# Seven-product operands of w_out2: made in tiles 1 to 10 of the first layer instead of in tile 11 and pair 0; two splits moved at each pair's end

## The chip, the cores and the metric

The kernel runs on one core of a Trainium2 chip. The metric is the device time of one execution in microseconds (us), and of several runs the median. A core has five engines with an instruction queue each, which are told apart by the names of the profile: PE (TensorE, matrix products; PEld are its weight loads), DVE (VectorE), ACT (ScalarE), POOL (GpSimd) and SP (SyncE, which issues all the DMA transfers of this kernel). Each queue is worked off in order; engines wait for each other by semaphores.

## What is computed

A small attention, a gated layer and a second layer with a leaky activation, over 8 x 576 = 4608 tokens of width 512, all in float32:

```python
p_packed = sm_attn(p, k, v)                 # 8 batches, 8 heads, 32 packed keys, head width 64
out = sm_attn(q, p_packed, p_packed)        # 576 tokens a batch
x = out.transpose(0, 2, 1, 3).reshape(4608, 512)
xn = x / sqrt(mean(x * x) + 1e-6) * rms_g
y = (silu(xn @ w_gate) * (xn @ w_val)) @ w_out          # 1536 hidden
h = y @ w_in2                                           # 2048 hidden
result = (maximum(h, 0) + alpha * minimum(h, 0)) @ w_out2
```

## The kernel before

**Precision.** A float32 operand is split in two float32r halves: `split_hi` (ACT, line 110) rounds it, `split_lo` (DVE, line 113) subtracts the rounded part. A product is then three matmuls (`mm3`, lines 121 to 124). In the profile the halves are `hh`/`hl`, `yh`/`yl`, `in_h`/`in_l`, `wgh`/`wgl`.

**First layer, tiles 0 to 11.** Tokens go in 12 tiles (variable `c`, line 949) of 512 (tiles 0, 4, 7, 10; "wide") or 320 (the others; "narrow"). Each tile walks 12 blocks `f` of the hidden width. A block is: product g (`blk_in`), Tanh on ACT and `s` on DVE (lines 1075, 1080; both read PSUM), product v, `s` times v (line 1084), `hsplit`, then the output product of the block before (`blk_out(f - 1)`) and the operand of the next one (`both`: `in_h` on ACT; `in_l` on POOL at line 385 in tiles 1 to 6, and loaded from memory at line 383 from tile 7 on). Between these stand bits of the attention of later tiles (`work(f, at)` with `at` from 1 to 4, and `burst`): transposes, maxima, exponentials. g, v and the attention share four PSUM banks in turn.

**The weights of the second layer.** `w_in2` and `w_out2` arrive with a representation that must be narrowed first (`narrow`: two operations on DVE, one on ACT, an addition on POOL of line 234). The second layer multiplies 2x2 blocks with seven products instead of eight, so that of each of the 8 block pairs of either matrix seven operands are needed, blocks and their sums and differences, each split and stored to memory (`sevenths`, line 290: seven products, that is a split on ACT, a split on DVE and a store from one of two buffers `w7o`, and four combinations on DVE at line 305; it gives way after each of its four steps). The generator `late` (`conv_late`) narrows all pairs, makes the operands of `w_in2` and stores the narrowed `w_out2` raw. It is called in `work(f, 3)` of tiles 1 to 10, lines 980 to 982: after each odd block of a narrow tile, after each block of a wide one, and twice for each fourth block there. The generator `making` (`make_o7`) loads the raw pairs of `w_out2` again and makes their operands: one step ahead of each block of tile 11 (line 1069), and in pair 0 of the second layer three steps in each turn (`make`, lines 1250, 1262, 1272).

**Second layer, pairs 0 to 4.** Each pair (variable `pr`, line 1219) has two rows of 512 tokens (pairs 0 to 2) or 384 (pairs 3 and 4). A turn `i` of 8 has seven products into three banks, whose sums and activations run on DVE (lines 1157, 1160, 1169) and ACT (lines 1164, 1165), and two output blocks out of a list `fill` of pieces that TensorE does later (blocks "a" and "c" of each turn; a block is 12 matmuls of 256 columns at 512 tokens). The 40 other output blocks and the last "c" block, c4, wait in the list `LATER` until the turns are over; the first three of it are b5 of turn 0, b5 of turn 1 and c4 of turn 7. `block` is a generator: its first step splits on ACT, its second on DVE and puts the matmuls into `fill`. At the end of the turns `next(splits[0])` and the loop over `LATER` (lines 1357 to 1374) split each block one ahead of its matmuls. Between them run `prep` of the next pair (lines 868 to 905, from `y_raw` loads) and the sums of the results. `load_next` streams the stored operands, one load for each that was used.

Of the kernel before, what the change touches and what calls it, by code (L numbers as in the profile page):

```python
# [8 lines left out]
F32 = mybir.dt.float32  # L9
F32R = mybir.dt.float32r  # L10
# [8 lines left out]
def attention_moe_moe2_kernel(ctx, tc, q, k, v, p, w_gate, w_val, w_out, rms_g, w_in2, w_out2, alpha, out):  # L19
    nc = tc.nc  # L20
# [5 lines left out]
    T = 512  # L26
# [14 lines left out]
    NST = 4  # L41
# [49 lines left out]
    y_dram = tc.dram_tile([KD, 128, NT], F32, name="y_dram")  # L91
    gv_dram = tc.dram_tile([NJ * 4, 128, 512], F32, name="gv_dram")
    lo_dram = tc.dram_tile([NF, 128, 512], F32, name="lo_dram")
    w_dram = tc.dram_tile([NP2, 128, 2, 512], F32, name="w_dram")
    w7_dram = tc.dram_tile([NP2 * 7, 128, 2, 256], F32, name="w7_dram")
    o7_dram = tc.dram_tile([NP2 * 7, 128, 2, 256], F32, name="o7_dram")

# [28 lines left out]
    with tc.manual_schedule():  # L126
# [124 lines left out]
        def conv_late():  # L251
            ahead = [load_wide(u, one, NST) for u in units2[:2]]
            yield
            for m in range(0, len(units2), 2):
                pair = []
                for n in (m, m + 1):
                    pair.append(one.tile([128, 4, 128], F32, tag="w32", name="w32", bufs=2))
                    steps = narrow(ahead.pop(0), pair[-1])
                    next(steps)
                    yield  # L260
                    for _ in steps:
                        pass
                    if n + 2 < len(units2):
                        ahead.append(load_wide(units2[n + 2], one, NST))
                kind, i = units2[m]
                if kind == "o2":
                    for e in range(2):
                        nc.sync.dma_start(out=w_dram[i, :, e], in_=pair[e].rearrange("p c x -> p (c x)"))
                yield
                if kind == "i2":  # L270
                    yield from sevenths(kind, i, [t.rearrange("p c x -> p (c x)") for t in pair])

        def make_o7():
            def raw_pair(i):
                t = one.tile([128, 2, 512], F32, tag="w64", name="o2_raw", bufs=NST)
                nc.sync.dma_start(out=t, in_=w_dram[i])
                return t

            ahead = [raw_pair(0)]
            yield  # L280
            for i in range(NP2):
                t = ahead.pop(0)
                for n, _ in enumerate(sevenths("o2", i, [t[:, e] for e in range(2)])):
                    if n == 1 and i + 1 < NP2:
                        ahead.append(raw_pair(i + 1))
                    yield

        seventh_tags = [["w7o"]]

        def sevenths(kind, i, pair):  # L290
            blocks = [t[:, h * 256:(h + 1) * 256] for t in pair for h in range(2)]
            b11, b12, b21, b22 = blocks
            kept = w7_dram if kind == "i2" else o7_dram

            def products(*which):
                for n, src in which:
                    tags = seventh_tags[0]
                    t = one.tile([128, 2, 256], F32R, tag=tags[0], name="w7o", bufs=2)
                    tags.append(tags.pop(0))
                    split_hi(t[:, 0], src)  # L300
                    split_lo(t[:, 1], src, t[:, 0])
                    nc.sync.dma_start(out=kept[i * 7 + n], in_=t.bitcast(F32))

            def combine(out, x, y, op=ALU.subtract):
                nc.vector.tensor_tensor(out=out, in0=x, in1=y, op=op)

            if kind == "i2":
                products((0, b11), (1, b12))
                yield
# [639 lines left out]
        for c, (t0, n, cuts) in enumerate(CH):  # L949
# [9 lines left out]
            def work(f, at):  # L959
                live = [ch for ch in chains["k"] if ch.kind is not None][:1] + chains["q"]  # L960
                swap = c > 0 or at == 3 and any(ch.kind == X or ch.kind == M for ch in live)
                if swap and c == 0:
                    preload(ACTF.Exp)
                for ch in live:
                    n_ = 0
                    while n_ < 2:
                        if ch.kind == R and (at == 1 or at > 2 and (ch is first[0] or n_ == 0)):
                            pass
                        elif n_ == 0 and ch.kind == E and (c == 0 or at < 4) or swap and ch.kind in (X, M):
                            pass  # L970
                        else:
                            break
                        ch.last = (c, f, at)
                        ch.next()
                        n_ += 1
                if swap and c == 0:
                    preload(ACTF.Silu)
                if c == 0:
                    conv(2 if at < 4 else 0)
                elif not last and at == 3 and (f % 2 or n == T):  # L980
                    for _ in range(1 + (n == T and f % 4 == 3)):
                        next(late, None)

            def q_turn(now, free):
                for n_, ch in enumerate(chains["q"]):
# [64 lines left out]
            for f in range(NF):  # L1050
# [9 lines left out]
                if last:  # L1060
                    if f == 0:
                        y_rows.append(load_rows(0, 0))
                        prepare = prep(0)
                        making = make_o7()
                    if f > 0:
                        next(prepare, None)
                    if f in (2, 3, 8, 9, 10):
                        next(prepare, None)
                    next(making)
                    if f > 2:  # L1070
                        load_next()
                tg = blk_in(f, 0, "g")
# [22 lines left out]
                    work(f, 4)  # L1095
                if f < NF - 1:
                    both(("o", f + 1))
            tail = [NF - 2, NF - 1]
            if nq:
                for ch in chains["q"]:  # L1100
# [29 lines left out]
            if c == NP1 - 2:  # L1130
                ap_ctx.close()
                p2 = ctx.enter_context(tc.tile_pool(name="p2", bufs=1, side="right", reuse_waits="tile"))
                for _ in late:
                    pass

# [45 lines left out]
                for x in "hl"  # L1181
            ]

        seventh_tags[0] = ["w7o", "w32"]
        acc = {}

        def make(pr, i):
            if pr == 0 and i < NP2 - 1:
                next(making, None)

        def banks(x, j):
            if (x, j) not in acc:
# [26 lines left out]
        for pr, (t0, w) in enumerate(PAIRS):  # L1219
# [4 lines left out]
            def copies(to, x, w=w):  # L1224
                for j, m in pieces(w):
                    to[j] = temp(m)
                    evac(to[j], banks(x, j)[:, 0:m], True)

            for i in range(NP2):
                if i == NP2 - 2 and not final:  # L1230
                    y_rows.append(load_rows(pr + 1, 0))
# [15 lines left out]
                for f_ in waiting:  # L1247
                    f_()
                prod(c_, 4, True)
                make(pr, i)  # L1250
                prod(b_, 6, False)
                u3 = temp(w)
                add2(u3, m1, b_)
# [5 lines left out]
                prelu(g11, n11, i)  # L1259
                n22 = halves_of(h22, h22, w)  # L1260
                prelu(h22, n22, i + NP2)
                make(pr, i)
                fill.pop(0)()
                prod(c_, 2, False)
                h12 = temp(w)
# [1 line left out]
                then = (lambda f_=copies, to=m1s: f_(to, "a")) if i == NP2 - 1 else None  # L1267
                for _ in block("a", 0, i, g11, w, i == 0, i == NP2 - 1, then):
                    pass
                n12 = halves_of(h12, h12, w)  # L1270
                prod(b_, 3, False)
                make(pr, i)
                h21 = keep(1, i, w)
                add2(h21, m1, b_)
                prelu(h12, n12, i)
                s1 = temp(w)
                add2(s1, h12, h22)
                s2, s3 = keep(2, i, w), keep(3, i, w)
# [2 lines left out]
                n21 = halves_of(h21, h21, w)  # L1281
                late_h[i] = (h22, h21, s2, s3)
                fill.pop(0)()
                waiting = [
                    lambda h=h21, n=n21, f=i + NP2: prelu(h, n, f),
                    lambda s=s1, i=i, w=w: list(block("c", 4, i, s, w, i == 0, i == NP2 - 1)),
# [51 lines left out]
                    after.pop(0)  # L1338

            prepare = iter(()) if final else prep(pr + 1)  # L1340
            splits = []
            for x, n, i in LATER:
                h22, h21, s2, s3 = late_h[i]
                g = {5: s2, 2: s2, 6: s3, 3: h22, 1: h21, 4: s1}[n]
                then = None
                if n == 4:
                    then = lambda: copies(m5s, "c")
                elif i == NP2 - 1:
                    then = {5: done_b6, 2: done_c, 6: done_b7, 3: done_d, 1: done_a}[n]
                splits.append(block(x, n, i, g, w, n in (5, 3) and i == 0, i == NP2 - 1, then))  # L1350

            def combine_next(k_):
                if k_ < len(LATER) and LATER[k_][1] == 2:
                    _, h21, s2, _ = late_h[LATER[k_][2]]
                    less2(s2, h21, s2)

            next(splits[0])
            for k_ in range(len(LATER)):
                combine_next(k_ + 2)
                if k_ + 1 < len(LATER):  # L1360
                    next(splits[k_ + 1])
# [46 lines left out]
```

## Time and profile before

| | us |
|---|---|
| three runs | 1677.40, 1678.57, 1680.42 |
| median | 1678.57 |
| the profiled execution | 1682.31 |
| its span, first to last instruction | 1680.5 |
| PE busy / DVE busy / ACT busy / POOL busy | 1587.7 / 1198.7 / 894.5 / 206.3 |
| tiles 1 to 10, by the profile | 167.4 to 870.1 |
| tile 11 | 870.1 to 932.0 |
| pairs 0, 1, 2, 3, 4 begin at | 932.0, 1110.7, 1270.4, 1430.8, 1554.9 |
| from one 128x256 matmul of an output block to the next (1212.83, 1212.95, 1213.07) | 0.12 |

All times inside the profiled execution count from its first instruction. A stage is told by the first Tanh of its tile (line 1075) or the first copy of its pair (line 1243). A row of the profile names the line, the engine, the operation and the tiles it writes and reads; tiles of one name are one kind, with buffer numbers left out, and some names are shortened by the profile (`w` is any weight tile, `w_dram` and `o_dram` the memory in which operands are kept). "[1.15 <-DVE A L647]" behind a row says how long the engine stood idle before it and what ended that. A busy engine is not an engine that works at its best: the matmuls overlap, and their length follows the granted clock.

### The profile page before, as it was taken

Reading aid. Unit: us, or ns where it says so; the run is one execution under the profiler, and the core shown is the slowest. Engines: PE = TensorE matmul, PEld = TensorE weight load, DVE = VectorE, ACT = ScalarE, POOL = GpSimd, SP = SyncE. Lnnn points to the kernel's source line nnn. Section 1 sums busy time; section 2 is a strip of 40 time slices with the busy share of each in tenths; the row PEclk is TensorE's granted clock in tenths of the full one; section 3 lists DMA queues with packets and bytes.
Section 4 is the critical chain, followed back from the end, with each engine's and each line's share of the span. In section 5 each row is a group of like instructions: output and inputs, shape, how many; then the busy total and the mean of one; then the engine's idle time right before and its main releaser. Section 6 shows DMA issues by size and latency. Waiting matters only on the chain.

```text
span 1680.5 us, 31955 instructions
## 1 busy us (share of the span) xinstructions
PE 1587.7 (94%) x11786; PEld 1391.8 (83%) x11786; DVE 1198.7 (71%) x2308; ACT 894.5 (53%) x1906; POOL 206.3 (12%) x174
## 2 busy tenths in 40 slices
PE   7789999999999999999997988999999999999999
PEld 5457887887778878888777777998898889999999
DVE  4786657767676676666646878967786788788776
ACT  4566555555455554555444555554654555555564
POOL 1442222323233310101000000000000000000000
PEclk8799999999999999999999999999999999999999
DMA  9876565646565465765436878666777667778876
GB/s 253 254 239 194 164 176 152 170 128 184 157 186 172 148 222 186 230 200 178 150 126 222 290 261 288 204 224 192 203 231 214 203 178 240 254 254 277 262 239 199
DMA packets 233883, 348.94 MB, mean 208 GB/s; under 512 B 62848, under 2 KB 96640, under 8 KB 233728
## 3 DMA queue, kind: packets, MB, share of 16 engines
q1 hardware_dynamic: 233728, 346.90, 66.1%
q8 instruction: 94, 1.54, 0.4%
q14 instruction: 61, 0.50, 0.1%
HBM read 284.96 MB, written 61.87 MB: 206 GB/s over the span
## 4 chain that ended last, share of the span: by engine, by line
PE 67%; DVE 17%; ACT 8%; DMA 4%; issue 3%; SPq 1%; POOL 0%; DVEq 0%; ACTq 0%; POOLq 0%
PE ps_g L122 11%; PE ps_g L124 10%; PE ps_g L123 10%; PE ps_y L122 8%; PE ps_y L123 7%; PE ps_y L124 7%; PE ps_wg L754 3%; DVE hl L113 2%; PE ps_v L122 2%; PE ps_v L123 2%; PE ps_v L124 2%; ACT hh L110 1%; DVE s L1084 1%; DMA o_dram<-w7o 1%; DVE w7o L113 1%
## 5 line engine op out<-in xcount | busy, mean ns | idle before, releaser
L122 PE MATMUL ps_g<-yh,w 128*128 128x512 f32 (+1 forms) x560 | 209.5, 374 | 12.4 <-DVE tmp L1157 11.5
L122 PE MATMUL ps_y<-hh,in_h 128*128 128x320 f32 (+1 forms) x576 | 209.0, 363 | 11.9 <-ACT hh L110 11.9
L123 PE MATMUL ps_g<-yl,w 128*128 128x512 f32 (+1 forms) x560 | 208.4, 372 | 0.0
L124 PE MATMUL ps_g<-yh,w 128*128 128x512 f32 (+1 forms) x560 | 207.5, 371 | 0.0
L123 PE MATMUL ps_y<-hl,in_h 128*128 128x320 f32 (+1 forms) x576 | 198.4, 345 | 2.9 <-DVE hl L113 2.1
L124 PE MATMUL ps_y<-hh,in_l 128*128 128x320 f32 (+1 forms) x576 | 196.5, 341 | 0.6 <-DMA in_l<-lo_dram 0.6
L110 ACT ACTIVATE hh<-kept 128x512 fp32r<-128x512 f32 (+1 forms) x200 | 117.1, 588 | 109.8 <-PE ps_g L123 59.6
L110 ACT ACTIVATE hh<-s 128x320 fp32r<-128x320 f32 (+1 forms) x144 | 75.6, 525 | 175.2 <-DVE s L1084 174.9
L122 PEld LDWEIGHTS ps_y<-hh,in_h 128*128 128x128 f32 x576 | 110.1, 191 | 65.6 <-issue 43.2
L124 PE MATMUL ps_y<-w,hl 128*128 128x256 f32 x576 | 163.7, 284 | 0.4 <-DVE hl L113 0.2
L123 PE MATMUL ps_y<-w,hh 128*128 128x256 f32 x576 | 162.8, 283 | 0.0
L122 PE MATMUL ps_y<-w,hh 128*128 128x256 f32 x576 | 162.5, 282 | 0.0
L1080 DVE SCALAR_TENSOR_TENSOR s<-s,ps_g 128x320 f32<-128x320 f32 (+1 forms) x132 | 71.1, 539 | 109.5 <-ACT s L1075 109.4
L124 PE MATMUL ps_g<-w,hl 128*128 128x256 f32 x432 | 124.8, 289 | 8.4 <-DVE hl L113 8.4
L113 DVE TENSOR_TENSOR hl<-kept,hh 128x512 fp32r<-128x512 f32 (+1 forms) x200 | 123.2, 631 | 13.4 <-ACT hh L110 12.0
L122 PEld LDWEIGHTS ps_g<-yh,w 128*128 128x128 f32 x560 | 106.4, 190 | 28.3 <-DVE tmp L1157 14.9
L113 DVE TENSOR_TENSOR hl<-s,hh 128x320 fp32r<-128x320 f32 (+1 forms) x144 | 82.1, 570 | 60.7 <-ACT hh L110 60.7
L122 PE MATMUL ps_g<-w,hh 128*128 128x256 f32 x432 | 124.6, 289 | 0.5 <-ACT hh L110 0.5
L123 PE MATMUL ps_g<-w,hh 128*128 128x256 f32 x432 | 124.3, 288 | 0.0
L385 POOL TENSOR_TENSOR in_l<-w_raw,in_h 128x512 fp32r<-128x512 f32 x72 | 95.0, 1320 | 231.4 <-ACT in_h L110 195.9
L1157 DVE TENSOR_TENSOR tmp<-tmp,ps_g 128x512 f32<-128x512 f32 (+2 forms) x140 | 88.2, 630 | 49.1 <-PE ps_g L124 48.6
L123 PEld LDWEIGHTS ps_y<-hl,in_h 128*128 128x128 f32 x576 | 110.6, 192 | 13.0 <-DVE hl L113 6.5
(196 smaller groups left out, 4198.5 us busy)
## 6 DMA issues: line engine op xcount, KB each, us to landing
w<-w_dram SPq DMA_DIRECT2D x280, 256.0 KB, 3.3
w<-o_dram SPq DMA_DIRECT2D x280, 256.0 KB, 3.0
gv_raw<-gv_dram SPq DMA_DIRECT2D x168, 256.0 KB, 3.9
in_l<-lo_dram SPq DMA_DIRECT2D x59, 256.0 KB, 4.0
w<-in_moe_w_out_dram SPq DMA_DIRECT2D x28, 512.0 KB, 5.2
w_dram<-w7o SPq DMA_DIRECT2D x56, 256.0 KB, 2.9
o_dram<-w7o SPq DMA_DIRECT2D x56, 256.0 KB, 2.5
vt<-in_v_dram SPq DMA_DIRECT2D x16, 576.0 KB, 5.7
```

Source lines behind the costliest of these rows:

```text
L110: nc.scalar.activation(out=hi, in_=src, func=ACTF.Copy)
L113: nc.vector.tensor_tensor(out=lo, in0=src, in1=hi.bitcast(F32), op=ALU.subtract)
L122: nc.tensor.matmul(out=o, lhsT=lh, rhs=rh, start=first, stop=False, skip_group_check=more)
L123: nc.tensor.matmul(out=o, lhsT=lh, rhs=rl, start=False, stop=False, skip_group_check=more)
L124: nc.tensor.matmul(out=o, lhsT=ll, rhs=rh, start=False, stop=last, skip_group_check=more)
L385: nc.gpsimd.tensor_tensor(out=l, in0=raw[u], in1=h.bitcast(F32), op=ALU.subtract)
L754: nc.tensor.matmul(out=ts[g][h * NP:(h + 1) * NP, :], lhsT=ppG[b][e * D:(e + 1) * D, c_, :], rhs=us[c_][e * D:(e + 1) * D, :], start=True, ...
L1080: nc.vector.scalar_tensor_tensor(out=s, in0=s, scalar=1.0, in1=tg, op0=ALU.add, op1=ALU.mult)
L1084: nc.vector.tensor_tensor(out=s, in0=s, in1=tv, op=ALU.mult)
L1157: nc.vector.tensor_tensor(out=out, in0=x, in1=y, op=ALU.add)
```

## The change

- `conv_late` makes the operands of `w_out2` as it makes those of `w_in2`, right after narrowing each pair. Storing and loading the raw `w_out2` goes, and with it `make_o7`, its calls in tile 11 and `make` in pair 0.
- The call of `late` moves from `work(f, 3)` to the end of each block, behind `both`, in tiles 1 to 10: one call a block in every tile, 120 in all. The generator needs 114 (one at the start, seven for each of 16 pairs, one to end).
- The four combinations of a pair, for both matrices, go from DVE to POOL.
- In the last turn of each pair of the second layer the first two blocks of `LATER` are split: on ACT right after block "a", on DVE after the activation of `h12`. Their matmuls go to `fill` there, and one more piece of `fill` is put out at the end of the turn. The loop over `LATER` begins at the third block. The order in which TensorE takes the pieces stays.

```diff
-    w_dram = tc.dram_tile([NP2, 128, 2, 512], F32, name="w_dram")
...
                 kind, i = units2[m]
-                if kind == "o2":
-                    for e in range(2):
-                        nc.sync.dma_start(out=w_dram[i, :, e], in_=pair[e].rearrange("p c x -> p (c x)"))
-                yield
-                if kind == "i2":
-                    yield from sevenths(kind, i, [t.rearrange("p c x -> p (c x)") for t in pair])
-
-        def make_o7():
...
+                yield
+                yield from sevenths(kind, i, [t.rearrange("p c x -> p (c x)") for t in pair])
...
-                    t = one.tile([128, 2, 256], F32R, tag=tags[0], name="w7o", bufs=2)
-                    tags.append(tags.pop(0))
+                    t = one.tile([128, 2, 256], F32R, tag="w7o", name="w7o", bufs=2)
...
             def combine(out, x, y, op=ALU.subtract):
-                nc.vector.tensor_tensor(out=out, in0=x, in1=y, op=op)
+                nc.gpsimd.tensor_tensor(out=out, in0=x, in1=y, op=op)
...
-                elif not last and at == 3 and (f % 2 or n == T):
-                    for _ in range(1 + (n == T and f % 4 == 3)):
-                        next(late, None)
...
-                        making = make_o7()
...
-                    next(making)
...
                     both(("o", f + 1))
+                if 0 < c < NP1 - 1:
+                    next(late, None)
...
-        def make(pr, i):
-            if pr == 0 and i < NP2 - 1:
-                next(making, None)
...
+            def later_block(k_, w=w, late_h=late_h):
...
+            splits = []
             for i in range(NP2):
...
                 for _ in block("a", 0, i, g11, w, i == 0, i == NP2 - 1, then):
                     pass
+                if i == NP2 - 1:
+                    splits += [later_block(k_) for k_ in range(2)]
+                    for sp_ in splits:
+                        next(sp_)
                 n12 = halves_of(h12, h12, w)
                 prod(b_, 3, False)
-                make(pr, i)
                 h21 = keep(1, i, w)
                 add2(h21, m1, b_)
                 prelu(h12, n12, i)
+                for sp_ in splits:
+                    next(sp_)
                 s1 = temp(w)
...
                 fill.pop(0)()
+                if i == NP2 - 1:
+                    fill.pop(0)()
...
-            next(splits[0])
-            for k_ in range(len(LATER)):
+            next(splits[2])
+            for k_ in range(2, len(LATER)):
```

## Rows read from the trace of the kernel before

**Rows 1.** The page, part 1: busy us of each engine, share of span, instructions.
```profile
PE 1587.7 (94%) x11786; PEld 1391.8 (83%) x11786; DVE 1198.7 (71%) x2308; ACT 894.5 (53%) x1906; POOL 206.3 (12%) x174
```

**Rows 2.** Windows: length, busy of PE, PEld, DVE, ACT, POOL; clock, DMA share, GB/s.
```profile
167.40:870.10 702.70, 678.29 (x5803) 575.71 (x5803) 463.74 (x996) 368.23 (x867) 151.47 (x125) 0.99 0.55 171
870.10:932.00 61.90, 48.26 (x274) 43.63 (x273) 41.48 (x88) 29.24 (x68) 0.00 (x0) 0.94 0.71 240
932.00:1110.70 178.70, 165.21 (x1001) 147.14 (x1000) 143.91 (x251) 97.17 (x188) 0.00 (x0) 0.96 0.78 258
1110.70:1270.40 159.70, 157.76 (x1009) 143.82 (x1009) 124.33 (x192) 85.56 (x148) 0.00 (x0) 1.00 0.70 211
...
592.00:676.10 84.10, 83.66 (x707) 68.81 (x705) 58.78 (x121) 43.85 (x96) 8.34 (x7) 1.00 0.61 197
sum 529.50, PE 510.09 PEld 436.81 DVE 357.06 ACT 284.91 POOL 118.12; mean PE 127.52 PEld 109.20 DVE 89.26 ACT 71.23 POOL 29.53
```

**Rows 3.** TensorE's waits, us in total, times, longest: tile 11; then pair 0.
```profile
PE ps_y L122 <- ACT hh L110: 11.9, 5, 5.2
PE ps_g L122 <- DVE s L1080: 0.9, 1, 0.9
...
PE ps_g L122 <- DVE tmp L1157: 11.5, 8, 2.3
```

**Rows 4.** Operations on `w7o` and of line 305, ns min/median/max: making of `w_out2`.
```profile
L113 DVE TENSOR_TENSOR w7o<-o_raw,w7o x56: 415/418/426, 877.9 to 1033.0; 128x256 fp32r<-128x256 f32 x56
...
L305 DVE TENSOR_TENSOR o_raw<-o_raw x32: 415/422/427, 883.5 to 1030.0; 128x256 f32<-128x256 f32 x32
```

**Rows 5.** Timeline of tile 11: start, us, engine, line, tiles, idle before and why.
```profile
877.41 0.72 ACT L110 ACTIVATE w7o<-o_raw 128x256 fp32r<-128x256 f32 x2 [2.19 <-DMA o_raw<-w_dram]
...
880.16 0.41 PE L122 MATMUL ps_y<-hh,in_h 128*128 128x320 f32 x1 [3.82 <-ACT hh L110]
...
905.38 0.42 ACT L110 ACTIVATE w7o<-o_raw 128x256 fp32r<-128x256 f32 x1 [5.70 <-DMA o_dram<-w7o]
```

**Rows 6.** Timeline of tiles 4 and 10; windows with the clock (last columns) behind stalls.
```profile
434.97 0.42 ACT L110 ACTIVATE w7o<-w 128x256 fp32r<-128x256 f32 x1 [4.33 <-DMA w_dram<-w7o]
...
436.54 0.24 PE L713 MATMUL ps_at<-ident,s 64*128 64x64 f32 x1 [1.71 <-ACT E1T L117]
...
815.74 1.82 PE L677 MATMUL ps_at<-ppbd,A2T 64*128 64x128 f32 x16 [2.00 <-DVE A L647]
...
437.40:440.80 3.40, 3.40 (x42) 2.69 (x31) 2.54 (x6) 1.20 (x2) 0.87 (x1) 0.51 0.64 192
...
1372.70:1376.10 3.40, 3.40 (x19) 3.40 (x18) 3.40 (x7) 1.04 (x2) 0.00 (x0) 0.50 0.25 74
```

**Rows 7.** Timeline of pair 1's end, and TensorE's waits from pair 1 on.
```profile
1206.92 0.63 ACT L1164 ACTIVATE neg<-tmp 128x512 f32<-128x512 f32 x1 [0.89 <-DVE tmp L1157]
...
1211.63 1.28 DVE L113 TENSOR_TENSOR hl<-kept,hh 128x512 fp32r<-128x512 f32 x2
...
1212.37 0.39 PE L124 MATMUL ps_g<-w,hl 128*128 128x256 f32 x1 [1.86 <-DVE hl L113]
...
PE ps_g L124 <- DVE hl L113: 6.6, 4, 1.9
PE ps_g L122 <- ACT hh L110: 0.5, 2, 0.3
```

**Rows 8.** Timeline of tile 2; lines 1080 and 305, ns min/median/max.
```profile
262.66 1.47 DVE L113 TENSOR_TENSOR w7o<-w,w7o 128x256 fp32r<-128x256 f32 x2
...
262.24 1.28 POOL L385 TENSOR_TENSOR in_l<-w_raw,in_h 128x512 fp32r<-128x512 f32 x1 [3.25 <-ACT in_h L110]
...
264.35 0.84 PE L677 MATMUL ps_at<-ppbd,A2T 64*128 64x128 f32 x9 [1.15 <-DVE A L647]
...
L1080 DVE SCALAR_TENSOR_TENSOR s<-s,ps_g x132: 467/487/689, 167.8 to 930.5; 128x320 f32<-128x320 f32 x96, 128x512 f32<-128x512 f32 x36
...
L305 DVE TENSOR_TENSOR w<-w,w x16: 411/424/1518, 238.6 to 814.7; 128x256 f32<-128x256 f32 x16
```

More of the change, by code (lines that the diff above doesn't have):

```diff
@@ L265, in conv_late @@
                 kind, i = units2[m]
-                if kind == "o2":
-                    for e in range(2):
-                        nc.sync.dma_start(out=w_dram[i, :, e], in_=pair[e].rearrange("p c x -> p (c x)"))
                 yield
-                if kind == "i2":
-                    yield from sevenths(kind, i, [t.rearrange("p c x -> p (c x)") for t in pair])
-        def make_o7():
[L274 to L279, printed above, removed]
-            yield
[L281 to L288, printed above, removed]
+                yield from sevenths(kind, i, [t.rearrange("p c x -> p (c x)") for t in pair])
         def sevenths(kind, i, pair):
@@ L296, in products @@
                 for n, src in which:
-                    tags = seventh_tags[0]
-                    t = one.tile([128, 2, 256], F32R, tag=tags[0], name="w7o", bufs=2)
-                    tags.append(tags.pop(0))
+                    t = one.tile([128, 2, 256], F32R, tag="w7o", name="w7o", bufs=2)
                     split_hi(t[:, 0], src)
@@ L1132, in attention_moe_moe2_kernel @@
                 p2 = ctx.enter_context(tc.tile_pool(name="p2", bufs=1, side="right", reuse_waits="tile"))
+                assert next(late, late) is late
                 for _ in late:
@@ L1182, in split_tiles @@
             ]
-        seventh_tags[0] = ["w7o", "w32"]
         acc = {}
-        def make(pr, i):
-            if pr == 0 and i < NP2 - 1:
-                next(making, None)
         def banks(x, j):
@@ L1227, in copies @@
                     evac(to[j], banks(x, j)[:, 0:m], True)
+            def later_block(k_, w=w, late_h=late_h):
+                x, n, i = LATER[k_]
+                then = None
+                if n == 4:
+                    g, then = s1, lambda: copies(m5s, "c")
+                else:
+                    h22, h21, s2, s3 = late_h[i]
+                    g = {5: s2, 2: s2, 6: s3, 3: h22, 1: h21}[n]
+                    if i == NP2 - 1:
+                        then = {5: done_b6, 2: done_c, 6: done_b7, 3: done_d, 1: done_a}[n]
+                return block(x, n, i, g, w, n in (5, 3) and i == 0, i == NP2 - 1, then)
+            splits = []
             for i in range(NP2):
@@ L1261, in attention_moe_moe2_kernel @@
                 prelu(h22, n22, i + NP2)
-                make(pr, i)
                 fill.pop(0)()
@@ L1269, in attention_moe_moe2_kernel @@
                     pass
+                if i == NP2 - 1:
+                    splits += [later_block(k_) for k_ in range(2)]
+                    for sp_ in splits:
+                        next(sp_)
                 n12 = halves_of(h12, h12, w)
                 prod(b_, 3, False)
-                make(pr, i)
                 h21 = keep(1, i, w)
@@ L1283, in attention_moe_moe2_kernel @@
                 fill.pop(0)()
+                if i == NP2 - 1:
+                    fill.pop(0)()
                 waiting = [
@@ L1340, in attention_moe_moe2_kernel @@
             prepare = iter(()) if final else prep(pr + 1)
[L1341 to L1350, printed above, removed]
+            splits[2:2] = [later_block(2)]
+            splits += [later_block(k_) for k_ in range(3, len(LATER))]
             def combine_next(k_):
```

## Prediction

> **What bounds it now.** I first read the engines' busy times: TensorE is busy 1587.7 of 1680.5 us [rows 1], the others less. So the time is TensorE's work, plus its idle time, plus what a lowered clock costs, and the question is where those two lie. The second view is busy time and granted clock by stage [rows 2]. Tiles 1 to 10 of the first layer take 702.7 us with TensorE idle for 24.4 (702.7 - 678.3). The last tile takes 61.9 us with 13.6 idle, at a mean clock of 0.94. Pair 0 of the second layer takes 178.7 with 13.5 idle at 0.96; pair 1, the same work at the same width, 159.7 with 1.9 idle. The third view is TensorE's waits in the two slow stages: in the last tile 11.9 us on ScalarE's `hh` and 0.9 on VectorE, in pair 0 eight waits of 11.5 us on VectorE's `tmp` [rows 3]. Both stages contain what the others lack, the making of the `w_out2` operands.
>
> Of that making two groups show the size [rows 4]: 56 splits on VectorE of 418 ns (with 56 on ScalarE about as long, and 56 stores) and 32 combinations of 422 ns. In pair 0 run 21 of its 32 product steps, 5.25 of 8 blocks: 5.25 x 11 x 0.42 = 24 us of VectorE, in a stage where it is 81% busy (143.9 of 178.7). In the last tile run 11. At 905.38 ScalarE had waited 5.7 us for a store to free one of the two `w7o` buffers [rows 5]; TensorE's longest wait, 5.2 us, follows [rows 3].
>
> A stall can cost twice. After TensorE's wait of 1.71 us at 436.54 the granted clock is 0.51 for 3.4 us, and after the stall that ends pair 2 it is 0.50 for as long: the 1.2 GHz level [rows 6]. At half rate 3.4 us of work lose 1.7 us. Not every stall does it: pair 1 has a clock of 1.00 with a wait of 1.86 us in it [rows 2, 7].
>
> **1. Last tile (number 11).** Gone are 19 products (a split on ScalarE, a split on VectorE and a store each), 12 combinations and four loads of raw pairs. Its five `hh` waits are 11.9 us. The longest, 5.2, goes whole with the store that caused it. The one of 3.82 at 880.16 goes in part: ScalarE waited before it for `y_raw`, which stays, and then 2.19 us for the raw pair, which goes [rows 5]; I keep 1.2. Of the other three and the VectorE wait (3.8 in all) I keep 0.9. That takes away 10.7, and with it the lowered clock, 0.06 x 61.9 = 3.7, of which I take 3.4 (two windows). The operands of pair 0 are still prepared here, now in a denser tile: I give back 2. Sum -12, bounds -14 and -8.
>
> **2. Pair 0.** Without the 21 steps its loop is pair 1's: 178.7 - 159.7 = 19.0. Only its first two deferred pieces differ, outputs of the last tile in place of blocks, 320 columns to a matmul in place of 256; by the idle-free tiles I allow 0.7 for them. Sum -18.3, bounds -16 and -19. What comes next there are pair 1's waits, and pair 1 shows none before its end.
>
> **3. Pair ends.** At the end of pair 1 the third matmul of the first deferred block waits 1.86 us for `hl`, which VectorE starts at 1211.63 [rows 7], behind `tmp`, two `kept` and a `kept` in its queue. Pairs 0 and 2 show the same, pairs 3 and 4 1.42, and 0.25 for `hh`. After the change the first two deferred blocks are split ahead of those four operations. ScalarE fits the two splits into the 0.89 us that it waits at 1206.92, and is 0.25 late after them. VectorE's two `hl` then start four operations of 0.65 earlier, near 1209.0 + 0.25, before TensorE needs the first at 1210.4. Late next is the third block, c4: its `hl` is seventh in that row, done near 1213.7. TensorE comes to it after two more blocks of 12 matmuls 0.12 us apart (the table above), near 1213.2. So 0.5 us of 1.86 stays, and by the same count at 384 columns 0.8 of 1.67: 3 x 1.36 + 2 x 0.87 = 5.8 us. Clock windows stand behind the ends of pairs 2 and 3 as well (1.7 each; pair 0's is in term 2); that so short a wait brings none is an assumption. Sum -9.2, bounds 0 (the wait moves whole to c4) and -12.
>
> **4. Tiles 1 to 10, what goes.** Now 87 calls of the making stand there: 6 in a tile of 320 tokens, 15 in one of 512, three of those doubled. A doubled call wants four products from two buffers. At 434.97 ScalarE waited 4.33 us for the store and TensorE then 1.71; before 815.74, in tile 10, TensorE waited 2.00 [rows 6]. With 0.2 us more behind the first and a clock window behind each that is 7.3 us, and one call to a block ends it: -7.3. Next, at 264.35 TensorE waits 1.15 us for transpositions on VectorE that stand behind two product splits, which took 1.47 us while GpSimd subtracted `in_l` [rows 8]. I find five such stalls, 4.8 us together. The call now stands behind that work and no longer delays transpositions: -4. Sixteen stores of raw `w_out2` go as well.
>
> **5. Tiles 1 to 10, what comes.** 56 splits on ScalarE (23 us), 56 on VectorE less the 32 combinations of `w_in2` (56 x 0.418 - 32 x 0.422 = 9.9 us), 64 combinations on GpSimd, 56 stores on SP's queue. GpSimd's 128x512 subtraction takes 1.28 us [rows 8]; for half the elements I estimate 0.65, so 42 us on an engine with 551 us free (702.7 - 151.5). The transfers are 40 more of 256 KB, 10.5 MB on 171 GB/s x 702.7 us = 120 MB [rows 2]. The call is now the last of a block. Queued behind it on ScalarE and VectorE is the next block's `s`, for which TensorE's next g bank waits; behind its stores on SP stand the `in_l` loads, which are needed a block later. Bounds: nothing, since tile 7 ran 15 calls with 0.4 us idle (84.1 - 83.7); above, all the idle time of the seven narrow tiles once more, as each gets twice its calls: 529.5 - 510.1 for these with tile 7, less 0.4, is 19.0 [rows 2]. In tiles 1 to 6 the splits of a call start under the `in_l` subtraction of the same block. I take 9, near the middle: more than half of the 19 has other causes, but a call in each block leaves less room.
>
> The Trainium skill (SBUF — State Buffer, "Who interferes with whom") speaks against moving combinations to GpSimd: a VectorE operation with two SBUF inputs and a GpSimd operation that reads SBUF exclude each other for a whole instruction. The trace agrees: a combination of 424 ns takes up to 1518, while `s`, which reads PSUM, is never over 689 [rows 8]. By that rule 64 x 0.65 = 42 us would be the most that the moved combinations could cost, and the sum would be near no change.
>
> **Sum.** -12 - 18.3 - 9.2 - 7.3 - 4 + 9 = -41.8 against the profiled execution's 1682.3 gives 1640.5. The median is 3.7 below that execution: 1637.
>
> **Rivals.**
> A, the wait only moves to c4, term 3 at zero: 1646. For it, c4's `hl` is seven operations away; against it, two blocks of cover come for two operations. 10%.
> B, the exclusion decides. `both` now puts the `in_l` subtraction right ahead of each call of tiles 1 to 6, and 4 calls in 7 make products. At 4.8 / 5 = 0.96 us for each of those 41 calls it is 39 us instead of 9: 1667. For it: all five stalls were this meeting. Against: what waits is now `s`, which had room where a transposition had none. 8%.
> C, slower: the store wait moves with the work. The last tile is the only place with a call in every narrow block, and there 11 calls with products lost 13.6 + 3.4 = 17 us, 1.55 each. With 48 such calls in the narrow tiles that is 74 us in place of their 19, while terms 1 to 3 and the 7.3 give 46.8: 1678.6 + 55 - 46.8 = 1687. It turns slower at 1.4 us a call. For it: a narrow block lasts (529.5 - 84.1) / 84 = 5.3 us, and a store can hold a buffer longer. Against: about half of the 17 us came of `y_raw`, raw pairs and the preparation. 5%.
> D, not what it says: the 120 places don't hold the 114 calls, and the rest runs in one stretch before tile 11. By the count they do; ten calls left over at 1.55 would give 1653. 1%.
>
> **Numbers.** The forecast (1623 to 1646) has 70%, A 10%, B 8%, C 5%, D 1%, and 6% stand for a price of term 5 between the forecast and B. The low end is term 5 at nothing and the better bounds of 1 and 3: 1637 - 9 - 2 - 3 = 1623. The high end is A together with term 5 at 20: 1637 + 9 + 11 = 1657. 0.2% is about what can be told from no change; faster holds the forecast, A, B and what is between them, 0.94; same 0.02; slower 0.04.
>
> **What would show it.** Right: the last tile near 50 us, pair 0 within 2 us of pair 1, no wait for a store in tiles 4 and 10, no wait of the first deferred block and a short one of c4, tiles 1 to 10 between 690 and 710 us. Wrong: ScalarE waiting for stores of `w7o` in tiles 8 and 9; VectorE splits of 1 us and more with waits for `s` behind them; pair 0 still 5 us above pair 1.

## The result

The changed kernel takes 1653.93 us (median of four, 1652.57 to 1659.08); the ratio to the kernel before is 0.9856 with a 95% interval of 0.9832 to 0.9879. That is faster by 1.4%, inside the range of 1623 to 1657, and 17 us above the 1637 that were predicted. The profiled execution took 1654.3 us with a span of 1652.5. Line numbers of the changed kernel differ: 109 and 112 are the splits, 361 the `in_l` subtraction, 281 the combinations, 1051 and 1055 the operations on `s`.

Busy time by stage in the changed kernel, columns as in [rows 2]: tiles 1 to 10, tile 11, pair 0, pair 1, and then tiles 3, 6 and 4 alone.

```profile
165.40:887.20 721.80, 686.09 (x5803) 577.77 (x5803) 501.49 (x1020) 384.23 (x922) 204.63 (x189) 0.99 0.57 181
887.20:931.20 44.00, 41.87 (x268) 39.56 (x267) 30.64 (x57) 23.26 (x50) 0.00 (x0) 1.00 0.58 201
931.20:1090.10 158.90, 158.31 (x1007) 144.08 (x1006) 124.99 (x194) 85.99 (x151) 0.00 (x0) 1.00 0.68 209
1090.10:1249.00 158.90, 158.31 (x1009) 143.92 (x1009) 124.24 (x192) 85.63 (x149) 0.00 (x0) 1.00 0.70 213
...
309.90:385.90 76.00, 66.57 (x567) 58.40 (x566) 55.30 (x109) 37.65 (x101) 27.45 (x25) 0.93 0.46 135
538.60:609.60 71.00, 60.98 (x541) 53.78 (x540) 53.23 (x105) 36.15 (x97) 26.72 (x25) 0.98 0.54 176
385.90:472.10 86.20, 85.81 (x729) 70.93 (x729) 60.51 (x112) 44.01 (x97) 27.65 (x24) 1.00 0.54 161
```

Against [rows 2], tile 11 fell from 61.9 to 44.0 us, pair 0 from 178.7 to 158.9, the very time of pair 1. Tiles 1 to 10 rose from 702.7 to 721.8. Divided by width, from the same starts of tiles, the three wide ones fell from 257.3 to 249.1 and the seven narrow ones rose from 445.4 to 472.7, tiles 3 and 6 most (66.5 to 76.0, 62.2 to 71.0). About 5 us of tile 3's 76.0 are a lowered clock: its mean is 0.93, with three stretches of 3.4 us at the lower of TensorE's two levels (1.2 GHz). So the whole account is -17.9 (tile 11), -19.8 (pair 0), -7.4 (pairs 1 to 4, 569.8 to 562.4), +19.1 (tiles 1 to 10), and -2.0 ahead of tile 1: 28.0 of span. The code ahead of tile 1 is the same in all kernels here, and tile 1 began between 165.4 and 170.1 us in them; that spread of some us is in every comparison of whole times below, so stages are compared first.

TensorE's waits in the changed kernel (us in total, times, longest): the first ones of tiles 1 to 10, then tile 11, then all pairs.

```profile
PE ps_at L653 <- DVE A2T L642: 6.1, 2, 3.3
PE ps_y L122 <- DVE hl L112: 3.4, 6, 0.7
PE ps_g L121 <- ACT ps_at L677: 2.6, 4, 1.0
...
PE ps_y L121 <- ACT hh L109: 1.7, 2, 1.2
...
PE ps_y L123 <- DVE hl L112: 2.3, 6, 0.6
```

The waits of [rows 3] are gone but for 1.7 us. In tiles 1 to 10 there are many small ones, on VectorE and on ScalarE work that stood behind VectorE. One of them, in tile 3, VectorE, GpSimd and TensorE in turn (start, length, then as in [rows 5]):

```profile
334.41 1.17 DVE L634 TENSOR_SCALAR s<-s 128x16 f32<-128x16 f32 x1
335.62 0.25 DVE L635 RECIPROCAL s<-s 128x16 f32<-128x16 f32 x1
335.79 1.61 DVE L112 TENSOR_TENSOR w7o<-w,w7o 128x256 fp32r<-128x256 f32 x2
337.32 0.68 DVE L637 TENSOR_TENSOR A<-A,s 128x512 f32<-128x512 f32 x1
337.92 0.47 DVE L1051 SCALAR_TENSOR_TENSOR s<-s,ps_g 128x320 f32<-128x320 f32 x1
...
334.26 1.29 POOL L361 TENSOR_TENSOR in_l<-w_raw,in_h 128x512 fp32r<-128x512 f32 x1 [4.47 <-ACT in_h L109]
335.49 0.76 POOL L281 TENSOR_TENSOR w<-w,w 128x256 f32<-128x256 f32 x1
336.33 0.79 POOL L281 TENSOR_TENSOR w<-w 128x256 f32<-128x256 f32 x1
...
338.45 0.67 PE L437 MATMUL ps_at<-kT,pT 64*32 64x288 f32 x2 [1.83 <-DVE s L1051]
```

An operation on 128x16 values, 0.17 us elsewhere, takes 1.17 while GpSimd subtracts `in_l`; two splits of 0.42 each take 1.61 while it combines; `s` comes late, and TensorE waits 1.83 us for the bank that `s` frees. At the end of tile 6 the two splits of a call stand right behind a subtraction:

```profile
596.70 1.30 POOL L361 TENSOR_TENSOR in_l<-w_raw,in_h 128x512 fp32r<-128x512 f32 x1 [3.34 <-ACT in_h L109]
596.96 2.18 DVE L112 TENSOR_TENSOR w7o<-w,w7o 128x256 fp32r<-128x256 f32 x2 [2.03 <-ACT w7o L109]
599.07 0.47 DVE L1051 SCALAR_TENSOR_TENSOR s<-s,ps_g 128x320 f32<-128x320 f32 x1
...
599.59 0.42 PE L121 MATMUL ps_g<-xh,wgh 128*128 128x320 f32 x1 [1.10 <-DVE s L1051]
599.85 0.32 PE L122 MATMUL ps_g<-xl,wgh 128*128 128x320 f32 x1
600.01 0.31 PE L123 MATMUL ps_g<-xh,wgl 128*128 128x320 f32 x1
```

They take 2.18 us in place of 0.84, and TensorE waits 1.10 for the `s` behind them. I call **excess** the time by which VectorE's operations exceed the median of their line, operation and shape, summed over all that do so by more than 0.1 us (computed from the trace). In tiles 1 to 10 it is 22.3 us before and 56.7 after, 46.2 of it in tiles 2 to 6. Of the 56.7, 41.0 us belong to operations that ran beside an `in_l` subtraction (19.1 before) and 8.8 to operations beside a combination.

### The profile page after: what moved, and what is told of

Same layout as the page of the kernel before. It is cut to its first block, busy times and chain, and to the rows that moved or that the text cites. A ratio compares the mean times of both kernels' runs of the same rounds, so it can differ in the third digit from the quotient of the medians.

```text
span 1652.5 us, 31947 instructions
## 1 busy us (share of the span) xinstructions
PE 1577.0 (95%) x11786; PEld 1381.3 (84%) x11786; DVE 1205.9 (73%) x2244; ACT 893.2 (54%) x1906; POOL 259.5 (16%) x238
## 4 chain that ended last, share of the span: by engine, by line
PE 66%; DVE 19%; ACT 7%; issue 3%; DMA 3%; SPq 1%; POOL 0%; DVEq 0%; ACTq 0%; POOLq 0%
PE ps_g L121 11%; PE ps_g L122 11%; PE ps_g L123 11%; PE ps_y L121 8%; PE ps_y L123 7%; PE ps_y L122 7%; DVE hl L112 3%; DVE s L1055 2%; PE ps_wg L730 2%; ACT hh L109 2%; DVE w7o L112 2%; PE ps_v L121 2%; PE ps_v L122 2%; PE ps_v L123 2%; DVE s L1051 1%
## 5 line engine op out<-in xcount | busy, mean ns | idle before, releaser
L121 PE MATMUL ps_g<-yh,w 128*128 128x512 f32 (+1 forms) x560 | 206.5, 369 | 0.0
L123 PE MATMUL ps_g<-yh,w 128*128 128x512 f32 (+1 forms) x560 | 205.7, 367 | 0.0
L121 PE MATMUL ps_g<-xh,wgh 128*128 128x256 f32 (+3 forms) x352 | 114.2, 325 | 14.7 <-ACT pT L116 4.1
L122 PE MATMUL ps_g<-w,hh 128*128 128x256 f32 x432 | 122.2, 283 | 0.0
L121 PE MATMUL ps_g<-w,hh 128*128 128x256 f32 x432 | 122.2, 283 | 0.0
```

The source lines that it names most:

```text
L121: nc.tensor.matmul(out=o, lhsT=lh, rhs=rh, start=first, stop=False, skip_group_check=more)
L122: nc.tensor.matmul(out=o, lhsT=lh, rhs=rl, start=False, stop=False, skip_group_check=more)
L123: nc.tensor.matmul(out=o, lhsT=ll, rhs=rh, start=False, stop=last, skip_group_check=more)
```

## The experiments

All are edits of the changed kernel, except where the kernel before is named. The lines shown are windows of tiles 1 to 10, columns as in [rows 2].

**The pair ends.** The early splits taken back out:

```diff
-                if i == NP2 - 1:
-                    splits += [later_block(k_) for k_ in range(2)]
...
-            for k_ in range(2, len(LATER)):
+            for k_ in range(len(LATER)):
```

> The changed kernel without the early splits at the end of the pairs (the loop over LATER begins at its first block, as before). By the prediction's term 3 this gives back 5.8 us of waits and up to three clock windows of 1.7: pairs 0 to 4 together 7 to 11 us longer than the changed kernel's 721.3, with a wait of about 1.86 us on hl at the end of pairs 0 to 2 and 1.4 at pairs 3 and 4. If the early splits only moved the wait, pairs 0 to 4 stay within 2 us of 721.3.

Measured: 1664.69 us, ratio to the kernel before 0.9905 (0.9878 to 0.9932). Pairs 0 to 4 took 729.6 against 721.3 us, 8.3 more, and the waits of before are back:

```profile
PE ps_g L123 <- DVE hl L112: 8.5, 5, 1.9
PE ps_g L121 <- ACT hh L109: 0.5, 2, 0.3
```

So term 3 holds: 8.3 where 9.2 were predicted. In the changed kernel c4 waits instead, shortly, as forecast: 0.39 in place of 0.12 us between two matmuls at 512 columns, an idle time of 0.58 at 384.

**Where the 19 us in tiles 1 to 10 come from.** Three theories stood: the exclusion between VectorE and GpSimd (P), VectorE's load (L), and the new place of the call (S). Three edits, one for each:

```diff
-                nc.gpsimd.tensor_tensor(out=out, in0=x, in1=y, op=op)
+                nc.vector.tensor_tensor(out=out, in0=x, in1=y, op=op)
```

> The changed kernel with the 64 combinations of sevenths on VectorE again instead of GpSimd. In the changed kernel tiles 1 to 10 take 721.8 us against 702.7 before, and VectorE operations there run 56.7 us over their medians in all, against 22.3 before. Theory P (exclusion: VectorE operations with two SBUF inputs stand still while GpSimd works): part of the 34 us comes from the combinations, 64 x 0.75 us on GpSimd, so the excess falls to about 35 us and tiles 1 to 10 to about 712. Theory L (load: VectorE simply has too much to do in narrow tiles): 64 x 0.42 = 27 us of VectorE more, so tiles 1 to 10 get slower, 725 to 735 us. Theory S (place: the call at the end of a block delays the next block's s): no change, 722 within 3.

```diff
+                elif not last and at == 3:
+                    next(late, None)
...
-                if 0 < c < NP1 - 1:
-                    next(late, None)
```

> The changed kernel with the call of late back in work(f, 3), but still one call for each block of tiles 1 to 10. Theory S (place): tiles 1 to 10 come back to about 705 us. Theory P (exclusion): the splits still meet GpSimd's in_l subtraction and its own combinations; tiles 1 to 10 stay within 5 of 722, and the waits move from s to the transpositions of the attention. Theory L (load): as P, 722 within 5.

```diff
-            if u[1] in have and steady[0] > NP1 - 6:
+            if u[1] in have and steady[0] > 1:
...
-            if steady[0] == NP1 - 6:
+            if steady[0] == 1:
```

> The changed kernel with in_l computed on GpSimd in tile 1 only, stored there, and loaded from memory from tile 2 on (in the changed kernel: computed up to tile 6, loaded from tile 7). It takes 60 subtractions of 1.29 us off GpSimd in tiles 2 to 6 and adds 60 loads of 256 KB. Theory P (exclusion): the excess of VectorE in tiles 2 to 6, now 46 us, falls to under 15, and tiles 2 to 6, now 369.9 us, to about 352; the whole to about 1637. Theory L and theory S: tiles 2 to 6 within 4 us of 370, as VectorE's own work and the place of the call are the same.

Measured, in this order:

```profile
167.30:895.20 727.90, 688.60 (x5803) 580.30 (x5803) 517.05 (x1084) 382.93 (x923) 155.04 (x125) 0.99 0.57 179
...
167.30:882.00 714.70, 684.03 (x5804) 579.46 (x5804) 474.21 (x1020) 385.29 (x923) 201.33 (x189) 0.99 0.58 183
...
168.30:870.40 702.10, 679.61 (x5803) 575.40 (x5803) 462.39 (x1020) 384.58 (x922) 122.78 (x129) 0.99 0.66 208
```

| | whole, us | ratio to before | tiles 1 to 10 | tiles 2 to 6 | excess |
|---|---|---|---|---|---|
| the kernel before | 1679.34 | 1 | 702.7 | 350.5 | 22.3 |
| the changed kernel | 1653.93 | 0.9856 (0.9832 to 0.9879) | 721.8 | 369.9 | 56.7 |
| combinations on VectorE | 1662.82 | 0.9893 (0.9873 to 0.9913) | 727.9 | 377.2 | 47.4 |
| call in its old place | 1649.12 | 0.9815 (0.9796 to 0.9835) | 714.7 | 359.5 | 26.6 |
| `in_l` loaded from tile 2 on | 1636.83 | 0.9740 (0.9719 to 0.9760) | 702.1 | 349.5 | 16.8 |

The stage times are of one execution each. How far two executions of the same code differ there, the kernel without the early splits shows: its tiles 1 to 10 are those of the changed kernel, and took 722.9 us for 721.8.

The third gives all of the 19 back, with the excess of tiles 2 to 6 at 6.4 us: the `in_l` subtraction on GpSimd is what the new calls ran into. The first went as L said: putting the combinations on GpSimd was a gain of 6.1 us here, although its excess falls a little without them. The second fell between: the place gave 7.1 of the 17 that S wanted, and the excess with it, so that place and exclusion had to be told apart.

**Meeting, or subtraction?** If the subtraction costs where a call's splits stand right behind it (M), then its order against the call matters, and nothing else of the place. The call was put ahead of `both`, the loading was tried in the kernel before, and with the loading the two places were tried again:

```diff
+                if 0 < c < NP1 - 1:
+                    next(late, None)
                 if f < NF - 1:
                     both(("o", f + 1))
-                if 0 < c < NP1 - 1:
-                    next(late, None)
```

> The changed kernel with the call of late at the end of each block put ahead of both(o, f + 1) instead of behind it. The same instructions on every engine, in_l still on GpSimd up to tile 6; only the order differs: the splits now come to VectorE before the in_l subtraction is put to GpSimd. Theory M (the meeting): the excess of VectorE in tiles 1 to 10 falls from 56.7 to about 30, tiles 1 to 10 from 721.8 to 708 to 714, the whole to about 1642. Theory G: the subtractions meet other VectorE work just as often, 722 within 4.

> The kernel before (combinations on VectorE, 87 calls in work(f, 3), w_out2 made late) with in_l computed on GpSimd in tile 1 only and loaded from memory from tile 2 on. In the changed kernel that same edit gave 17 us (1653.9 to 1636.8) and took tiles 2 to 6 from 369.9 to 349.5 us. Theory M (the meeting: the in_l subtraction costs only where a call's VectorE splits stand right behind it): the kernel before has few such meetings, five stalls of 4.8 us together, so it gets 3 to 7 us faster, 1672 to 1677, and its VectorE excess in tiles 1 to 10 falls from 22.3 to about 8. Theory G (GpSimd's subtractions are dear in themselves, as VectorE always meets them): a gain of 15 us or more as in the changed kernel, about 1663.

> The changed kernel with in_l loaded from tile 2 on and with the call of late back in work(f, 3), one a block. Alone the first gave 19.7 us in tiles 1 to 10 (721.8 to 702.1) and the second 7.1 (714.7). Theory M: both take away the same meeting, so together they give no more than the loading alone: tiles 1 to 10 at 702 within 4, the whole near 1637. If the place has a price of its own (the call delays s), they add up: about 695 and 1630.

> The changed kernel with in_l loaded from tile 2 on and the call of late ahead of both(o, f + 1). With in_l on GpSimd this order gave 9.0 us in tiles 1 to 10 (721.8 to 712.8). Theory M (that gain was the meeting of splits and subtraction): with the subtraction gone the order is worth nothing, tiles 1 to 10 at 702 within 3, the whole near 1637. If the order had a worth of its own, 693.

Measured, in this order:

```profile
165.60:878.40 712.80, 680.38 (x5803) 574.90 (x5803) 485.01 (x1020) 383.60 (x923) 202.72 (x189) 1.00 0.58 183
...
165.60:857.40 691.80, 672.20 (x5802) 571.27 (x5802) 445.62 (x996) 368.66 (x866) 71.79 (x65) 1.00 0.63 196
...
166.10:869.70 703.60, 679.82 (x5803) 574.67 (x5803) 457.33 (x1020) 387.53 (x923) 121.94 (x129) 1.00 0.67 208
...
170.00:869.10 699.10, 677.36 (x5803) 573.14 (x5803) 462.06 (x1020) 385.08 (x922) 122.71 (x129) 1.00 0.66 209
```

| | whole, us | ratio to before | tiles 1 to 10 | excess |
|---|---|---|---|---|
| call ahead of `both` | 1649.91 | 0.9824 (0.9808 to 0.9841) | 712.8 | 38.9 |
| kernel before, `in_l` loaded | 1670.05 | 0.9951 (0.9935 to 0.9968) | 691.8 | 6.2 |
| `in_l` loaded, old place | 1636.24 | 0.9748 (0.9734 to 0.9763) | 703.6 | 11.2 |
| `in_l` loaded, call ahead of `both` | 1637.58 | 0.9763 (0.9746 to 0.9780) | 699.1 | 16.5 |

The order alone gives 9.0 us in tiles 1 to 10, with the same instructions, as M said (708 to 714). That size is not firm: 3.4 of the 9.0 are two stretches of lowered clock fewer, and the profiled execution (1645.42) is the fastest of its four. By the medians the whole gains 4.0 us, and M's 1642 was missed, as was its 30 for the excess. What the order does to the splits is plain. Counted in the traces, of the 112 splits of `w7o` in tiles 1 to 10 of the changed kernel 30 are more than 0.1 us over their median under an `in_l` subtraction, by 25.4 us together. With the call ahead of `both` there are 8 (8.0 us), in its old place 7 (7.1 us), and in the kernel before 3 of 56 (2.5 us).

With `in_l` loaded the old place costs 1.5 us and the order gives 3.0, while the three whole times lie within 1.4 us: a price of the place itself is 3 us at most, and the rest of what it changed is the meeting. In the kernel before the loading gave 10.9 us in these tiles, where M said 3 to 7; 5.1 of them are three stretches of lowered clock (at 437.4, 550.1 and 816.3) that the execution with the loading does not have, and the other 5.8 are as M said. By the whole times the loading is worth 9.0 us there (1679.02 in the same comparison to 1670.05) and 17.1 in the changed kernel: about half of it was there before the change, and half came with it.

**What is left in narrow tiles.** With `in_l` loaded the narrow tiles take 453.0 us with 84 calls and 438.4 with 42 (the kernel before with `in_l` loaded); 5.1 of the difference are stretches of lowered clock that the latter's execution does not have. Is that 14.6 us the load of VectorE, the number of calls, or `w_out2`'s own work?

> The changed kernel with in_l loaded from tile 2 on and the 64 combinations on VectorE. It asks whether the combinations on GpSimd still help once the in_l subtraction is gone from there. If their gain (6.1 us in tiles 1 to 10 with in_l on GpSimd: 727.9 against 721.8) is VectorE's load alone, they help here as much: tiles 1 to 10 at 706 to 710 against 702.1, the whole near 1643. If the exclusion between combinations and VectorE matters, then without any GpSimd work beside narrowing the excess falls under 8 from 16.8 and the time is the same or better, 1632 to 1637.

Measured: 1643.37 us, 0.9790 (0.9776 to 0.9805), tiles 1 to 10 at 707.5 against 702.1, excess 11.8. Load again: 27 us of combinations on VectorE cost 5.4, though they meet less.

On top of the loading, half of the narrow tiles' calls were moved into the wide ones, whose blocks then make two each:

```diff
+                elif not last and at == 3 and n == T:
+                    next(late, None)
...
-                if 0 < c < NP1 - 1:
+                if 0 < c < NP1 - 1 and (n == T or f % 2):
```

> The changed kernel with in_l loaded from tile 2 on, and with the 114 calls of late placed otherwise: one behind each odd block of the narrow tiles (42, as before) and two in each block of the wide tiles (72), one in work(f, 3) and one at the block's end. With in_l loaded, narrow tiles take 438.4 us with 42 calls (the kernel before) and 453.0 with 84. Theory N (what is left is the number of calls in narrow tiles): narrow tiles at 438 to 442, wide tiles at 249 plus what two calls in a block cost there, 0 to 6; tiles 1 to 10 at 688 to 696, the whole near 1626. Theory W (w_out2's own work is dear wherever it stands, above all by the store waits of two buffers): the wide tiles take over the 14 us, tiles 1 to 10 at 700 or more.

Measured: 1655.54 us, 0.9862 (0.9837 to 0.9887). The narrow tiles came to 440.4, as N said; the three wide ones took 277.8 in place of 249.1, more than W said. So in the narrow tiles 12.6 of the 14.6 us go with the number of calls, with all of `w_out2`'s work still in the kernel; the whole missed N's 1626 by the wide tiles. The first three lines are these wide tiles, the others ScalarE's waits (total, times, longest):

```profile
371.30:472.20 100.90, 90.26 (x732) 71.55 (x731) 62.35 (x132) 49.05 (x114) 21.90 (x24) 1.00 0.70 224
596.00:688.00 92.00, 85.50 (x705) 69.12 (x704) 61.14 (x128) 48.02 (x111) 19.66 (x21) 0.99 0.64 217
800.20:885.00 84.80, 80.84 (x574) 65.74 (x574) 55.74 (x108) 44.69 (x98) 20.07 (x23) 1.00 0.53 183
...
ACT w7o L109 <- DMA w_dram<-w7o: 34.2, 15, 5.2
ACT w7o L109 <- DMA o_dram<-w7o: 14.0, 6, 3.7
```

48 us of waiting for the two `w7o` buffers: that is rival C's mechanism, and it takes two calls in a block of 7 us to bring it out. In the changed kernel ScalarE waits 5.3 us for them in all, in seven small waits.

Then fewer were moved: in tiles 3, 6 and 9 alone every second call is left out, and the wide tiles make a second one in each third block only.

```diff
+                elif not last and at == 3 and n == T and f % 3 == 2:
+                    next(late, None)
...
-                if 0 < c < NP1 - 1:
+                if 0 < c < NP1 - 1 and (c % 3 or f % 2):
```

> The changed kernel with in_l loaded from tile 2 on, where tiles 3, 6 and 9 have a call behind odd blocks only (18), the wide tiles one a block and a second in work(f, 3) of each third block (48), the other narrow tiles one a block (48). Tiles 3, 6 and 9 took 187.7 us with 36 calls and take 177.6 in the kernel before with in_l loaded. Theory N: they come back to about 178 to 180, the wide tiles stay at 249 to 252, tiles 1 to 10 near 695, the whole near 1629. Theory W: the wide tiles get longer by what tiles 3, 6 and 9 gain; 702.

Measured: 1635.16 us, 0.9744 (0.9724 to 0.9764). Tiles 3, 6 and 9 took 180.7 us in place of 187.7, the wide ones 250.2, tiles 1 to 10 696.0: N. The whole missed its 1629, for tile 11 took 46.5 in place of 44 (the making now ended with tile 10) and tile 1 began at 170.1.

**A version that is faster than both.** `in_l` loaded from tile 2 on, the call ahead of `both`, single calls spared in tiles 3 and 6 only (`c not in (3, 6) or f % 2`) and the second call in each third block of the wide tiles:

> What the runs before point to, in one kernel: the changed kernel with in_l loaded from tile 2 on, the call of late ahead of both, calls behind odd blocks only in tiles 3 and 6, and a second call in work(f, 3) of each third block of the wide tiles (120 places for 114 calls, so that the making ends half a tile before tile 11). Theory N: tiles 3 and 6 fall to 63 and 61 us from 65.7 and 65.4, tile 9 stays near 57, the wide tiles near 250; tiles 1 to 10 at 691 to 696 against 699.1 (in_l loaded, call ahead of both), tile 11 at 44 to 45, where it was 46.5 when the making ended with tile 10; the whole at 1628 to 1634. If the number of calls in tiles 3 and 6 is not what costs there, 1637.

Measured: 1629.21 us (five runs), ratio 0.9706 (0.9692 to 0.9720). Tile 3 at 62.9, tile 6 at 60.9, and:

```profile
169.10:864.50 695.40, 676.09 (x5803) 573.11 (x5803) 459.88 (x1020) 383.20 (x922) 122.82 (x129) 1.00 0.66 210
864.50:908.50 44.00, 41.88 (x268) 39.57 (x267) 30.64 (x57) 23.30 (x50) 0.00 (x0) 1.00 0.61 201
```

## Why the prediction was right, and where it was off

The time lies in the range of 1623 to 1657, but not in the forecast of 1623 to 1646 that had 70%: it came where 6% stood, at a price of term 5 between the forecast and B. The high end of the range had been made of rival A and of term 5 at 20, and neither came. In the profiled execution the narrow tiles took 22.3 us more than the sum says; terms 1, 2 and 4 and the start of tile 1 gave 10.3 us more than it says, and term 3 gave 1.8 less outside pair 0. That the time stayed in the range is in part luck.

**Term 1** was too small: 17.9 us for 12. The idle time that stays was right (2.1 us predicted and measured), the two clock windows went, and nothing was given back for the denser tile, which makes 2 us. Another 0.8 is idle time in gaps that the listed waits do not hold. 1.4 us is the border of the stages: six matmuls of 128x512 of pair 0, 0.23 us apart, stood in the window of tile 11 before and stand in that of pair 0 now. The rest is mostly a second wait that the list of TensorE's waits does not show. In the kernel before, in tile 11:

```profile
918.58 0.41 PE L122 MATMUL ps_y<-hh,in_h 128*128 128x320 f32 x1 [1.06 <-ACT hh L110]
919.10 0.42 PE L123 MATMUL ps_y<-hl,in_h 128*128 128x320 f32 x1
919.36 0.31 PE L124 MATMUL ps_y<-hh,in_l 128*128 128x320 f32 x1
919.50 0.31 PE L122 MATMUL ps_y<-hh,in_h 128*128 128x320 f32 x1
...
918.56 0.49 DVE L113 TENSOR_TENSOR hl<-s,hh 128x320 fp32r<-128x320 f32 x1 [0.54 <-ACT hh L110]
919.10 0.19 PEld L123 LDWEIGHTS ps_y<-hl,in_h 128*128 128x128 f32 x1 [0.34 <-DVE hl L113]
...
PEld ps_y L123 <- DVE hl L113: 2.8, 9, 0.3
PEld ps_y L122 <- DVE hl L112: 1.6, 5, 0.3
```

The second matmul comes 0.52 us behind the first, where the fourth comes 0.14 behind the third. Its weights are `hl`, which VectorE makes until 919.05, after `hh`, and the weight load waits 0.34 us for them while the first matmul counts as busy. The last two lines are these waits of weight loads in tile 11 (total, times, longest) before and after the change: 1.2 us less.

**Term 2** holds: pair 0 is pair 1 to a tenth, 19.8 for 18.3, of which 0.9 is its pair end (159.8 without the early splits) and it would be 1.4 more without the six matmuls that now stand in its window.

**Term 3** holds (8.3 for 9.2), and rival A is out: c4's wait is there, at the place that the count of VectorE's queue gave and somewhat shorter (0.3 and 0.6 us for 0.5 and 0.8).

**Term 4** holds for the doubled calls: the wide tiles lost 8.2 us for 7.3. The 4 us of transpositions can't be told from what came in their place.

**Term 5 failed.** With the 4 us, the narrow tiles should have lost 5 us net and lost 27.3, so that 9 was 31, and the bound of 19 was no bound. The step that failed is the bound: it took each new call to cost what a call had cost, and those had seldom met an `in_l` subtraction (3 lengthened splits). Term 5 saw that the splits would now start under it and set no price on that; the new place behind `both` made the meeting common (30). Rival B named that mechanism and gave 39 for it; it was given 8%. The runs divide the 27.3 in two: 14.6 us for 42 more calls without the subtraction from tile 2 on (453.0 against 438.4), and the other 12.7 with the subtraction there, of which the order alone takes 4 to 9 away. Of the signs named beforehand, tiles 1 to 10 left their 690 to 710, and VectorE splits of 1 us and more came, 28 of 112 (4 of 56 in the kernel before), with waits for `s` behind some; ScalarE's waits for stores in tiles 8 and 9 were 3.1 us.

The Trainium skill's rule (SBUF — State Buffer, "Who interferes with whom") agrees with this trace: the splits have two SBUF inputs, and two of them take 2.18 us in place of 0.84 beside GpSimd's subtraction and combination. The operation on 128x16 has one such input; it ends 0.03 us behind the subtraction (335.58, 335.55). The same section counts `tensor_scalar` among the operations that can contend, in a 2-port mode; no row shows in which mode this one ran. The price was not that of the combinations, to which the prediction's sentence on the rule had tied it: moved to GpSimd, where one takes 0.75 us in the median and 1.12 at most (0.65 was estimated), they lengthened VectorE operations by 8.8 us, took 27 us of work off VectorE, and gained 6.1 us with the subtraction there and 5.4 without. What cost was work that had been on GpSimd before, met more often.

Rival C is out at one call a block and true at two. Rival D is out: the second layer's operands were there, and pair 0 is pair 1.

What stays open: why tiles 3 and 6 pay most for the calls (+9.5 and +8.8 in the changed kernel, the other narrow ones 0 to +3.4). In tile 3 some 5 us of it are the lowered clock, in tile 6 nearly 7 are idle time of TensorE. Both have the most long splits (6 each) and few products of the `ps_wg` kind (16 matmuls, where tiles 2 and 5 have 96); no run tells these apart.

## What to carry over

A step that is moved should be costed against what stands next to it in its new place, on every engine and not on its own alone: the same instructions cost 4 to 9 us more behind a GpSimd subtraction than ahead of it. A bound that takes the present price of a step for the price of more such steps holds only where their neighbours stay the same. Where work has slack, look for the place that pays nothing (the wide tiles, one call a block), and check how soon its buffers come free before doubling it there.

## What was not expected of the hardware

A wait of TensorE for `hh` cost more than its idle time: the weight load of the next matmul then waited 0.34 us for `hl`, in time that counts as busy. Behind other waits little is lost: after the 1.10 us for `s` at 599.59 the matmuls come 0.26, 0.16 and then 0.14 us apart. A small VectorE operation on 128x16 values went from 0.17 to 1.17 us beside GpSimd's subtraction, so that also the short steps of a chain are hit, and not the long ones alone. `s`, which reads PSUM, was never over 691 ns in any run; where it came late, as at 337.92 and 599.07, the work ahead of it in VectorE's queue had been stretched.
